# Retention in blocks of 64 tokens on the four quarters of the matrix engine

## Chip, cores, metric

One core of one Trainium2 chip. The metric is the device time of one execution in microseconds (us), the median of several. PE is TensorE, the matrix engine; PEld are its weight loads; VectorE (DVE), ScalarE (ACT) and SP (which issues transfers) are the others.

## The reference, in short

```python
def _attn_ref(q, k, v):                       # (4, 8, 768, 64) each
    for t in range(S):
        state = gamma * state + k[t] (x) v[t] # per batch and head, 64x64
        y[t] = scale * q[t] @ state
# y as (3072 tokens, 512) feeds
h = x @ w_in                                  # 512 -> 2048
g = h * erf(softplus(h))
return g @ w_out                              # 2048 -> 512
```

The retention is the small part. The two large products, done by a scheme with seven products for eight, are the rest. Everything is fp32.

## The kernel before: the parts concerned

The retention is done by chunks of 128 tokens, 24 in all (6 for each of 4 sequences). Keys and queries are scaled so that no decay is left inside a chunk. Each chunk is one visit of PE between two parts of the large products:

```python
# L416, scores of the next chunk: contraction 64, 128 keys x 128 queries
nc.tensor.matmul(pp[s][:, hp, :], KT[j][s*D:(s+1)*D, hp, :], QT[j][s*D:(s+1)*D, hp, :], ...)
# L428, VectorE: causal mask, out of PSUM into SBUF, 2 x (128 x 512)
nc.vector.tensor_tensor(AM[j][:, s], SC[j][s], causal[...].to_broadcast([P, HP, C]), op=ALU.mult)
# L451, state times queries: 64 x 64, 128 columns, on four quarters
nc.tensor.matmul(place(h), state[own, u, :], QT[j][own, u, :], ...)
# L456, values times masked scores: contraction 128, 64 x 128
nc.tensor.matmul(place(h), V[j][:, h, :], AM[j][:, h % 2, h // 2, :], ...)
# L465, state update: contraction 128, 64 x 64
nc.tensor.matmul(new[...], KQ[j][:, 0, h, :], V[j][:, h, :], ...)
... # ScalarE copies the result to XC, VectorE adds `new` to the state
```

The order of one round g in the steady part:

```python
        hidden_part(g, 4)
        hidden_part(g, 3)          # its last read of a PSUM bank is on VectorE (L627)
        if more:
            O_(j)                  # L451, L456, L465
            A(j)                   # VectorE: state
            if j + 1 < NJ:
                S_(j + 1, ps_h)    # L416
                M(j + 1)           # L428
        ...
        for p in (2, 4):
            project_part(g - 1, p) # L674
        gate(g)
```

`ps_h` is a pool of two PSUM banks that the large products and the scores share in turn.

## Time and profile before

| | before |
|---|---|
| median of 3 runs (a fourth makes it 710.75 below) | 710.84 us |
| PE busy | 98% |
| VectorE, ScalarE busy | 53%, 36% |
| one round with a visit / without | 27.97 / 24.60 us |

PE is the bound, so read the chain of waits in order of time: each row is when a piece of PE's program started, how long until the next, which line, how many records (an fp32 matmul leaves two). A round is the distance between two rows of the same line and count.

### The profile page before, as it was taken

To read this page: it belongs to the slowest core of one execution; us is meant where nothing else is said; L and a number is where in the kernel's file an instruction comes from. 1 tells how busy PE (TensorE), PEld (TensorE's weight loads), DVE (VectorE), ACT (ScalarE), POOL (GpSimd) and SP (SyncE) were. 2 spreads that over 40 slices of the span, in tenths; PEclk is the share of its full clock that TensorE was granted. 3 is DMA by queue.
4 is the path that set the end of the run, shared out by engine and by line. 5 is a ranking of instruction groups with operands and counts; after the bars stand their busy time and mean duration, and the time that the engine had idled before them with its cause. 6 is when DMAs were issued, how large, how long until landed. Compare 5 with 4: busy or idle time off the path is not lost.

```text
span 709.3 us, 12055 instructions
## 1 busy us (share of the span) xinstructions
PE 695.8 (98%) x5126; PEld 590.8 (83%) x5126; DVE 379.4 (53%) x532; ACT 256.7 (36%) x289; POOL 6.2 (1%) x19
## 2 busy tenths in 40 slices
PE   8799999999999999999999999999999999999998
PEld 7535444486999998999999999989999999999996
DVE  4599999264854553563554454544553463243234
ACT  3266462325144144243242441441432423414431
POOL 1000000010000000000000000000000000000000
PEclk9999999999999999999999999999999999999999
DMA  9999763102322232211222223230321210000000
GB/s 193 209 255 245 185 193 61 26 1 42 102 38 37 71 60 43 60 32 30 62 42 43 67 37 60 55 59 9 57 57 32 44 48 1 2 30 1 1 30 30
DMA packets 147205, 46.96 MB, mean 66 GB/s; under 512 B 135760, under 2 KB 136016, under 8 KB 147152
## 3 DMA queue, kind: packets, MB, share of 16 engines
q1 hardware_dynamic: 144640, 45.66, 29.5%
q10 hardware_dynamic: 2512, 0.53, 0.5%
q8 instruction: 40, 0.66, 0.4%
q14 instruction: 13, 0.11, 0.1%
HBM read 39.86 MB, written 6.29 MB: 65 GB/s over the span
## 4 chain that ended last, share of the span: by engine, by line
PE 95%; DMA 2%; SPq 1%; DVE 1%; issue 0%; ACT 0%; POOL 0%; DVEq 0%; POOLq 0%
PE hp L602 35%; PE o L674 35%; PE o L545 8%; PE hp L532 7%; PE r L456 3%; PE hp L416 3%; DMA w_in_sb<-in_moe_w_in_dram 2%; PE r L451 1%; PE r L465 1%; PE o L362 1%; PE r L403 1%; SPq L114 1%; PE r L416 1%; SPq L156 0%; DVE am L428 0%
## 5 line engine op out<-in xcount | busy, mean ns | idle before, releaser
L602 PE MATMUL hp<-xs,w_in_sb 128*128 128x128 f32 x1280 | 149.8, 275 | 0.0
L602 PEld LDWEIGHTS hp<-xs,w_in_sb 128*128 128x128 f32 x1280 | 147.8, 192 | 1.6 <-issue 0.5
L674 PE MATMUL o<-w_out_sb,h 128*128 128x256 f32 x640 | 141.7, 379 | 0.0
L674 PEld LDWEIGHTS o<-w_out_sb,h 128*128 128x128 f32 x640 | 121.6, 190 | 16.5
L602 PE MATMUL hp<-xT,w_in_sb 128*128 128x128 f32 x960 | 113.7, 275 | 0.0
L602 PEld LDWEIGHTS hp<-xT,w_in_sb 128*128 128x128 f32 x960 | 111.9, 192 | 1.9 <-issue 1.0
L674 PE MATMUL o<-w_out_sb,e 128*128 128x256 f32 x480 | 112.1, 383 | 0.0
L521 DVE TENSOR_TENSOR e<-h,e 128x1024 f32<-128x1024 f32 x42 | 49.6, 1222 | 101.7 <-ACT e L502 101.7
L674 PEld LDWEIGHTS o<-w_out_sb,e 128*128 128x128 f32 x480 | 88.2, 190 | 12.5 <-PE r L456 0.2
L497 ACT ACT_TABLE_LOAD x24 | 30.8, 1283 | 79.1 <-issue 69.6
L532 PE MATMUL hp<-xT,w_in_sb 128*128 128x512 f32 x128 | 56.7, 596 | 1.8 <-DVE w_in_sb L218 1.4
L627 DVE TENSOR_TENSOR h<-h,hp 128x512 f32<-128x512 f32 x20 | 13.7, 687 | 75.3 <-PE hp L602 75.3
L532 PEld LDWEIGHTS hp<-xT,w_in_sb 128*128 128x128 f32 x128 | 23.8, 190 | 30.9 <-issue 27.7
L502 ACT ACTIVATE e<-e 128x2048 f32<-128x2048 f32 (+1 forms) x23 | 42.1, 1836 | 0.2
L497 ACT ACTIVATE e<-h 128x2048 f32<-128x2048 f32 x22 | 42.0, 1910 | 0.2
L615 DVE TENSOR_TENSOR h<-h,hp 128x512 f32<-128x512 f32 x20 | 13.8, 688 | 51.9 <-PE hp L602 51.9
L470 ACT COPY xT<-r 128x256 f32<-128x256 f32 x44 | 14.4, 375 | 66.7 <-PE r L465 58.9
L625 ACT COPY h<-hp 128x512 f32<-128x512 f32 x20 | 11.7, 585 | 60.3 <-PE hp L602 60.3
L620 ACT COPY h<-hp 128x512 f32<-128x512 f32 x20 | 11.7, 586 | 57.9 <-PE hp L602 57.9
L618 ACT COPY h<-hp 128x512 f32<-128x512 f32 x20 | 11.7, 585 | 55.3 <-PE hp L602 55.3
L502 ACT ACT_TABLE_LOAD x24 | 30.8, 1283 | 0.4
L613 ACT COPY h<-hp 128x512 f32<-128x512 f32 x20 | 11.7, 587 | 48.6 <-PE hp L602 48.6
(102 smaller groups left out, 655.3 us busy)
## 6 DMA issues: line engine op xcount, KB each, us to landing
w_out_sb<-in_moe_w_out_dram SPq DMA_DIRECT2D x14, 512.0 KB, 5.4
kq<-in_k_dram SPq DMA_DIRECT2D x24, 256.0 KB, 3.5
v<-in_v_dram SPq DMA_DIRECT2D x24, 256.0 KB, 3.3
w_in_sb<-in_moe_w_in_dram SPq DMA_DIRECT2D x12, 512.0 KB, 9.4
out_dram<-r SPq DMA_DIRECT2D x23, 256.0 KB, 2.3
kq<-in_q_dram SPq DMA_DIRECT2D x256, 16.0 KB, 1.8
kb<-in_k_dram SPq DMA_DIRECT2D x256, 16.0 KB, 1.7
w_out_sb<-in_moe_w_in_dram SPq DMA_DIRECT2D x4, 512.0 KB, 8.0
```

What stands on the lines that cost most here:

```text
L416: nc.tensor.matmul(pp[s][:, hp, :], KT[j][s * D : (s + 1) * D, hp, :], QT[j][s * D : (s + 1) * D, hp, :], start=True, stop=True,)
L456: nc.tensor.matmul(place(h), V[j][:, h, :], AM[j][:, h % 2, h // 2, :], start=(not c and h % 4 < 2), stop=True, skip_group_check=True,)
L470: nc.scalar.copy(XC[m][:, r::2, i * C : (i + 1) * C], pp[r][:, :2, :])
L497: nc.scalar.activation(E[g], HS[g], AF.Softplus)
L502: nc.scalar.activation(E[g][:, half], E[g][:, half], AF.Erf)
L521: nc.vector.tensor_tensor(E[g][:, half], HS[g][:, half], E[g][:, half], op=ALU.mult)
L532: nc.tensor.matmul(p, w_in_of(ft, kk), XC[0][:, kk, :], start=(kk == 0), stop=(kk == n_k - 1))
L545: nc.tensor.matmul(O[0][tt].rearrange("p (d c) -> p d c", d=2), E[g][:, u * TCH + tt * P : u * TCH + (tt + 1) * P], w_out_of(ft), start=(f ...
L602: nc.tensor.matmul(bank[:, u, :], w_in_sb[:, s, IN[a], kk, u * P : (u + 1) * P], XS[m][b][:, kk, :], start=(p in (1, 2, 5) and u == 0 and ...
L615: nc.vector.tensor_tensor(h["11"], h["11"], flat, op=ALU.add)
L627: nc.vector.tensor_tensor(h["12"], h["12"], flat, op=ALU.add)
L674: nc.tensor.matmul(O[m][i][:, half, :], G[g][a][:, u * P : (u + 1) * P], w_out_sb[:, s, OUT[b], u, :], start=i not in started, stop=(s == ...
```

## The change

The intent: a matmul of 64x64 leaves three quarters of the 128x128 array free, and four of them can run side by side. If every product of a visit is 64x64 with 64 columns, the array changes shape only on the way in and out; and in blocks of 64 tokens the upper-right quarter of the scores, which the mask would zero, is never computed. The price is twice as many matmuls, a state update in the middle of the chunk, and products that cross: where the token half of the keys and the target bank don't match, the values land in other banks ("crossed") and VectorE adds them. From chunk 7 on:

```diff
+    def sub_scores(j):            # 16 matmuls, into columns :D of two banks
+                    SC[j][s][t, hp, :D], KT[j][own, hp, t], QT[j][own, hp, t], start=True, stop=True,
+    def sub_mask(j):              # 2 x (128 x 256)
+                AM[j][:, s, :, :D], SC[j][s][:, :, :D], causal_d[...], op=ALU.mult,
... 
+    def sub_visit(j, g):
+        other = SC[j + 1] = [ret_psum(ps_h) for _ in range(2)]
+        def of_values(crossed):   # 8 matmuls
+                        other[a][own, u % 2, D:] if crossed else pp[a][own, u % 2, t],
+                        V[j][t, 2 * u + r, :], AM[j][t, r, u, :D],
+                        start=crossed or first(r, col), stop=True, skip_group_check=True,
...
+        if c:
+            of_state(0)
+        ...                       # state updates of both blocks, 16 matmuls (8 in a last chunk)
+            nc.vector.tensor_tensor(state, state, new[0], op=ALU.add)
+        of_values(False)
+        if j + 1 < NJ:
+            sub_scores(j + 1)
+            sub_mask(j + 1)
+        of_values(True)
+        of_state(1)
+        ...                       # ScalarE copies, VectorE adds the crossed values and new[1]
-        if more:
+        if more and not first:
+            sub_visit(j, g)
+        elif more:
             O_(j)
             A(j)
-                S_(j + 1, ps_h)
-                M(j + 1)
+            SC[j + 1] = [ret_psum(ps_h) for _ in range(2)]
+            sub_scores(j + 1)
+            sub_mask(j + 1)
```

Line numbers move: L602 becomes L712, L674 becomes L784, L627 becomes L737. New: L485 scores, L492 masks, L520 state times queries, L535 values, L556 state updates, L561 first addition to the state, L576 the addition of the crossed values.

More of the change, by code (lines that the diff above doesn't have):

```diff
@@ L304 @@
     )
+    causal_d = const.tile([P, D], F32, name="causal_d")
+    for r in range(2):
+        own = slice(r * D, (r + 1) * D)
+        nc.gpsimd.tensor_copy(causal_d[own], causal[own, own])
     state = const.tile([P, HP, D], F32, name="state")
@@ L471, in ret_out @@
         pace(2.5)
+    def sub_scores(j):
+        for hp in range(HP):
+            for a, s in itertools.product(range(2), range(2)):
+                t, own = slice(a * D, (a + 1) * D), slice(s * D, (s + 1) * D)
+                nc.tensor.matmul(
+                    SC[j][s][t, hp, :D], KT[j][own, hp, t], QT[j][own, hp, t], start=True, stop=True,
+                )
+    def sub_mask(j):
+        AM[j] = ret.tile([P, 2, HP, C], F32, name="am")
+        for s in range(2):
+            nc.vector.tensor_tensor(
+                AM[j][:, s, :, :D],
+                SC[j][s][:, :, :D],
+                causal_d[:, None, :].to_broadcast([P, HP, D]),
+                op=ALU.mult,
+            )
@@ new lines, in sub_visit, with first, of_state @@
+    def sub_visit(j, g):
+        c = j % NC
+        m, i = divmod(j, JPC)
+        if i == 0:
+            XC[m] = ret.tile([P, HP, TCH], F32, name="xT")
+        pp = [ret_psum() for _ in range(2)]
+        clear = set()
+        def first(*bank):
+            new = bank not in clear
+            clear.add(bank)
+            return new
+        def of_state(a):
+            t = slice(a * D, (a + 1) * D)
+            for u in PAIRS:
+                for r in range(2):
+                    col, own = u // 2, slice(r * D, (r + 1) * D)
+                    nc.tensor.matmul(
+                        pp[r][col * D : (col + 1) * D, u % 2, t], state[own, u, :], QT[j][own, u, t],
+                        start=first(r, col), stop=True, skip_group_check=True,
+                    )
+        other = SC[j + 1] = [ret_psum(ps_h) for _ in range(2)]
+        def of_values(crossed):
+            for u in PAIRS:
+                for a in range(2):
+                    r = 1 - a if crossed else a
+                    col, t = u // 2, slice(a * D, (a + 1) * D)
+                    own = slice(col * D, (col + 1) * D)
+                    nc.tensor.matmul(
+                        other[a][own, u % 2, D:] if crossed else pp[a][own, u % 2, t],
+                        V[j][t, 2 * u + r, :],
+                        AM[j][t, r, u, :D],
+                        start=crossed or first(r, col), stop=True, skip_group_check=True,
+                    )
+        if c:
+            of_state(0)
+        last = chunk_of(g - 1)
+        if (g - G0) % 2 == 1:
+            clear.update((("o", 0), ("o", 1)))
+        new = [
+            O[last][3][:, 1, :].rearrange("p (u d) -> p u d", d=D),
+            pp[1][:, 2:, :].rearrange("p a (b d) -> p (a b) d", d=D),
+        ]
+        adds = range(2) if c < NC - 1 else range(1)
+        for u in range(HP):
+            for r in range(2):
+                for a in adds:
+                    t, h = slice(a * D, (a + 1) * D), 2 * u + r
+                    nc.tensor.matmul(
+                        new[a][r * D : (r + 1) * D, u, :], KQ[j][t, 0, h, :], V[j][t, h, :],
+                        start=first("o" if a == 0 else 1, r), stop=True, skip_group_check=True,
+                    )
+        if c:
+            nc.vector.tensor_tensor(state, state, new[0], op=ALU.add)
+        else:
+            nc.vector.tensor_copy(state, new[0])
+        of_values(False)
[4 more added lines that the diff above has]
+        of_state(1)
+        for r in range(2):
+            a = 1 - r
+            x, y = XC[m][:, r::2, i * C : (i + 1) * C], other[a][:, :2, D:]
+            if c or a:
+                nc.scalar.copy(x, pp[r][:, :2, :])
+                x = x[:, :, a * D : (a + 1) * D]
+                nc.vector.tensor_tensor(x, x, y, op=ALU.add)
+            else:
+                nc.scalar.copy(x[:, :, D:], pp[r][:, :2, D:])
+                nc.scalar.copy(x[:, :, :D], y)
+        if c < NC - 1:
+            nc.vector.tensor_tensor(state, state, new[1], op=ALU.add)
@@ L828 @@
         hidden_part(g, 3)
-        if more:
+        if more and not first:
+            sub_visit(j, g)
+        elif more:
             O_(j)
             A(j)
-            if j + 1 < NJ:
-                S_(j + 1, ps_h)
-                M(j + 1)
+            SC[j + 1] = [ret_psum(ps_h) for _ in range(2)]
+            sub_scores(j + 1)
+            sub_mask(j + 1)
         if g + 1 < NG and (g - G0) % 2:
```

## The prediction

> **What bounds the kernel now.** I read the busy totals first, then the chain of work that ended last, then that chain in order of time around one visit of the retention, then the timeline and the single start times inside one visit.
>
> ```profile
> span 709.3 us, 12055 instructions
> ...
> PE 695.8 (98%) x5126; PEld 590.8 (83%) x5126; DVE 379.4 (53%) x532; ACT 256.7 (36%) x289; POOL 6.2 (1%) x19
> ```
>
> The matrix engine (PE) is busy all the time, VectorE half of it. The chain of waits says the same: 95% of it is PE, in program order. So time is gained only by making the stream of PE shorter, and lost by any hole in it. The retention comes in visits, one per chunk of 128 tokens; the chain in order of time (start us, us, what) shows one whole round with a visit, and a round after the last chunk, without one:
>
> ```profile
> 211.64 3.57 PE hp L602 x32
> 215.21 0.60 PE r L451 x16
> 215.81 1.02 PE r L456 x16
> 216.83 0.46 PE r L465 x16
> 217.30 1.09 PE hp L416 x16
> 218.39 10.56 PE o L674 x48
> ```
> ```profile
> 655.41 3.57 PE hp L602 x32
> 658.98 10.36 PE o L674 x48
> 669.35 8.93 PE hp L602 x80
> 678.28 1.73 PE o L674 x8
> 680.01 3.57 PE hp L602 x32
> ```
>
> L451 is query times state, L456 the masked scores times values, L465 the state update, L416 the next chunk's scores. A visit is 3.18 us, and the L674 block after it takes 10.56 instead of 10.36 us, so a visit costs 3.38 us. The change touches 17 visits (chunks 7 to 23): 57 us, 8% of the span, is all that is at stake.
>
> Each fp32 matmul leaves two records (x16 for 8 matmuls). By records, L465 (two column halves, 64 columns streamed) runs at 0.46/16 = 29 ns, the others at 37 (L451) to 68 ns (L416). The single start times show why. In L451, four quarters of 64x64: starts 243.266, .272, .279, .286, then .375: four within 20 ns, then the next four 109 ns later. In L465: pairs 7 ns apart, every 58.4 ns. At every border between kinds the next group comes some 0.15 us late: L451 is 4 groups x 0.109 = 0.44 us, the other 0.16 us is the change of array shape.
>
> The timeline (start us, us, engine, line) shows what VectorE does meanwhile:
>
> ```profile
> 215.25 0.69 DVE L627 TENSOR_TENSOR h<-h,hp 128x512 f32<-128x512 f32 x1 [3.99 <-PE hp L602]
> ...
> 217.75 0.42 DVE L484 TENSOR_TENSOR state<-state,r 128x256 f32<-128x256 f32 x1 [1.81 <-ACT xT L470]
> ...
> 218.42 1.29 DVE L428 TENSOR_TENSOR am<-hp,causal 128x512 f32<-128x512 f32 x2 [0.25 <-PE hp L416]
> ```
>
> The two masks of the scores (L428) run under the 10.56 us of L674. Nothing waits for them.
>
> **What the Trainium skill says.** "TensorEngine Tiling (Array Packing)", section "Key Properties": a change of tiling mode drains the engine, while tiles of one mode work independently and load weights in parallel. The trace agrees: 0.16 us at a border, four quarters side by side inside L451. "PSUM — Partial Sum Buffer", section "PSUM bank collisions raise a hardware error": guard PSUM by bank and quadrant with semaphores, not by address. This trace has no such wait inside a visit; the changed program has one (below). "TensorE: Matmul & The Clock Gate", section "Wait — 56ns, not 53.3ns?": starts are never closer than about 25 ns, however few columns. The trace differs for starts in different quarters, 7 ns, but in its mean over any eight records it never beats 27 ns, so as a mean rate this is untested. "Runtime: NRT & Kernel Launch", section "Instruction fetch mechanics": a floor of about 20 sequencer cycles per instruction. No stretch of this trace is long and dense enough to show or refute it.
>
> **The change part by part.** Removed per visit: 8 matmuls each of L451, L456, L465 and L416, 64 records in four array shapes. Added: 64 matmuls of 64x64 with 64 columns, 128 records: state times the first 64 queries (16), state updates of both blocks (32), own-block values (16), next scores (32), crossed values (16), state times the last 64 queries (16). Consecutive matmuls go to the four quarters in turn, and the two row halves write different banks. All are of one shape, so only the way in and the way out drain.
>
> PE's own time: 128/4 = 32 groups. A quarter streams 64 columns as in L465, so a group takes 58.4 ns (L465's pitch), if four quarters go side by side as in L451: 32 x 0.0584 = 1.87 us. Way in 0.16, way out 10.56 - 10.36 = 0.20. Sum 2.23 against 3.38 us: 1.15 us gained per visit, about 19 us in all, if nothing waits.
>
> But something waits. The crossed values are written into the unused columns of the very two banks that hold the new scores, directly after these scores. In the built program the first two crossed matmuls each carry a wait for VectorE, and counting VectorE's increments gives which: the first and the second mask of the new scores. Both masks, hidden before, now lie between two matmuls. Cost, from the trace of before:
> - last score matmul's start to the start of the mask: 246.081 to 246.38 = 0.30 us with a 272 ns matmul; with L465's 222 ns form 0.25 us;
> - the masks are 128x256 instead of 128x512: 0.42 us each (L484's form). Two of 0.69 us took 1.29, so the second starts 0.08 before the first ends: 0.34 + 0.42 = 0.76 us;
> - end of a VectorE instruction to PE: 0.055 us (seven starts of PE that a mask released early in the run: 0.053 to 0.057);
> - restart with an empty weight buffer 0.05 us, less the 0.058 us that the next group would have taken anyway.
>
> Sum 1.06 us of hole. The other waits don't bind by these numbers. The scores need L627 to have left their bank: 0.85 us after the visit's start, while PE comes to them after 64 records, 0.16 + 0.93 = 1.09 us. The addition to the state that the last products need is done at about 1.5 us, before the masks. Work moved to VectorE (two additions of 128 elements, one more to the state, smaller masks: +0.4 us a visit) finds it half idle. ScalarE's copies come about 1 us later, and the gate behind them with them; its consumer on PE comes two product blocks later.
>
> So a full visit costs 2.23 + 1.06 = 3.29 us against 3.38. There are 12 of them: -1.1 us. First chunks of a sequence (2) have no state product: 3.29 - 0.47 = 2.82 against 2.58 + 0.20 = 2.78, +0.1 us in all. Last chunks (2) have one update instead of two: 3.06 against 2.91, +0.3. The very last visit has no scores and no mask: 1.8 before, about 1.7 after, -0.1. In the visit ahead of the 17 only the scores change, from 1.09 to 0.16 + 0.47: -0.5. Sum: -1.3 us. The whole gain on the array goes into the wait for the masks; from 710.8 the time comes to 709.5 us.
>
> **The rivals.**
> 1. No wait: had the masks been hidden as before, 16 visits would gain 1.06 us more, 17 us: 692.5, faster by 2.6%. For it: the profile of before, where nothing waits for a mask inside the steady part. Against it: the wait stands in the program. I hold it very unlikely.
> 2. A floor of 25 ns per matmul as a mean, also across quarters. The 96 records ahead of the wait then take 2.40 instead of 1.40 us, the 32 behind it 0.80 instead of 0.47: +1.33 us a visit, +21 us: 731. For it: no stretch of before is denser than 27 ns. Against it: that is just what the array allows there (109/4), and starts are 7 ns apart.
> 3. The sequencer can't feed 256 instructions so fast. The queue holds 64 when the visit starts (the "TensorE" page's opening table); of the 192 ahead of the wait 128 must be fed. At 20 cycles of 1.2 GHz, 16.7 ns: 2.13 us instead of 0.16 + 1.40 = 1.56, and the hole refills the queue for the rest: +0.57 us, +9 us: 718.5. For it: density doubles. Against it: nothing measured here.
> 4. Weights of four quarters load only two at a time: 0.109 us a group, +1.6 us a visit, +26 us: 736. Against it: in L451 the first four loads start at 243.104 to .124 and the next four at 243.159 to .179, 55 ns later in every quarter.
>
> **Range and chances.** I give the sum (709.5) about 60%, rival 3 or a milder feed limit 22%, rivals 2 and 4 together 13%, rival 1 with other gains 5%. The middle of that lies a little above the sum: 711 us, with 704 to 729 to hold it 8 times in 10. Faster by over 2% (below 696.6) 0.05; within 2% 0.75; slower by over 2% (above 725) 0.20.
>
> **What would show each step.** In the chain of the changed kernel: groups of 16 records at 0.23 us (the array step; 0.40 would be rival 2, 0.44 rival 4; groups that start dense and thin out after some 32 pairs, rival 3). A wait of PE for the mask before the crossed values, about 1 us, some 16 times, where before it had none. The L674 block after a visit still 10.56 us. VectorE some 7 us busier, ScalarE the same. I would be wrong if that wait is short or missing, or if the 64x64 matmuls run clearly slower than 14.6 ns a record.

## More of the kernel before

Kernel before, three rounds around the border of a sequence:

```profile
295.54 3.57 PE hp L602 x32
...
323.04 3.57 PE hp L602 x32
...
350.41 3.57 PE hp L602 x32
...
378.37 3.57 PE hp L602 x32
```

The last chunk of a sequence (no state update) makes a round of 27.50 us, the first one (no state product) 27.37, a full one 27.96.

## The result, and the profile after

| | before | after |
|---|---|---|
| median of 4 runs | 710.75 us | 711.91 us |
| range | 710.15 to 711.07 | 711.67 to 712.89 |
| ratio | | 1.002, 95% interval 1.0003 to 1.0037 |

A ratio is the mean time of one kernel's fast runs over that of the other's in the same rounds, so not quite the ratio of the medians quoted. The result is correct and the time the same within 2%.

The busy totals of the page of the changed kernel:

```profile
PE 688.0 (97%) x6214; PEld 583.6 (82%) x6214; DVE 385.3 (54%) x581; ACT 256.9 (36%) x291; POOL 6.6 (1%) x21
```

PE is busy 7.8 us less, but the span of the profiled run is 711.2 instead of 709.3 us: PE now has holes. The chain of waits in order of time, one full round of the changed kernel:

```profile
239.99 3.57 PE hp L712 x32
244.65 0.54 PE hp L485 x32
245.19 0.42 DVE am L492
245.98 0.40 PE hp L535 x11
246.67 10.56 PE o L784 x48
257.23 8.93 PE hp L712 x80
266.16 1.73 PE o L784 x8
267.88 3.57 PE hp L712 x32
```

Two things to see. The round is 267.88 - 239.99 = 27.89 us, against 27.97. And in a chain that held only PE, a mask on VectorE now stands between the scores (L485) and the crossed values (L535). (Only the longest pieces are listed, so short ones leave gaps between rows.) The busy times in the three parts of that visit (us; then for each engine busy us and instructions; the clock) give the sizes:

```profile
243.49:244.92 1.43, 1.43 (x97) 1.43 (x96) 1.11 (x2) 0.00 (x0) 0.00 (x0) 1.00 0.00 0
244.92:245.98 1.06, 0.52 (x18) 0.25 (x8) 0.76 (x2) 0.00 (x0) 0.00 (x0) 1.00 0.21 50
245.98:246.67 0.69, 0.69 (x31) 0.62 (x31) 0.00 (x0) 0.00 (x0) 0.00 (x0) 1.00 1.16 261
```

The columns after the stretch are PE, PEld, DVE, ACT, POOL, then the granted clock, the DMA share and GB/s. First 96 matmul records (and one that was still running) in 1.43 us, dense. Then 1.06 us in which PE starts almost nothing (what it shows as busy is the modelled end of matmuls that had started) and VectorE spends 0.76 us on two instructions, the masks. Then the last 32 records and the way out. The list of waits has it for the whole run (us in total, times, longest):

```profile
PEld hp L535 <- DVE am L492: 10.7, 16, 0.7
PE hp L535 <- DVE am L492: 8.5, 16, 0.5
```

Sixteen times, once in each visit that has scores. The 8.5 us count only time with no matmul in flight; the loss is larger, because a matmul's modelled end covers the first part of each hole and PE restarts with one matmul, then waits again for the second mask.

### The profile page after: what moved, and what is told of

Read it like the earlier page. It is cut to its first block, busy times and chain, and to the rows that moved or that the text cites. A ratio compares the mean times of both kernels' runs of the same rounds, so it can differ in the third digit from the quotient of the medians.

```text
span 711.2 us, 14317 instructions
## 1 busy us (share of the span) xinstructions
PE 688.0 (97%) x6214; PEld 583.6 (82%) x6214; DVE 385.3 (54%) x581; ACT 256.9 (36%) x291; POOL 6.6 (1%) x21
## 4 chain that ended last, share of the span: by engine, by line
PE 90%; DVE 4%; DMA 3%; SPq 1%; issue 1%; ACT 0%; DVEq 0%
PE hp L712 35%; PE o L784 34%; PE o L655 8%; PE hp L642 4%; PE hp L535 2%; DMA w_in_sb<-in_moe_w_in_dram 2%; PE r L520 1%; PE hp L485 1%; DVE am L492 1%; PE o L556 1%; DMA w_out_sb<-in_moe_w_out_dram 1%; SPq L114 1%; DVE w_out_sb L211 1%; DMA kq<-in_q_dram 1%; PE r L535 1%
## 5 line engine op out<-in xcount | busy, mean ns | idle before, releaser
L712 PE MATMUL hp<-xs,w_in_sb 128*128 128x128 f32 x1280 | 149.8, 275 | 0.0
L712 PEld LDWEIGHTS hp<-xs,w_in_sb 128*128 128x128 f32 x1280 | 147.8, 192 | 1.6 <-issue 0.5
L784 PE MATMUL o<-w_out_sb,h 128*128 128x256 f32 x640 | 141.7, 379 | 0.0
L784 PEld LDWEIGHTS o<-w_out_sb,h 128*128 128x128 f32 x640 | 121.6, 190 | 16.5
L712 PE MATMUL hp<-xT,w_in_sb 128*128 128x128 f32 x960 | 113.7, 275 | 0.0
L712 PEld LDWEIGHTS hp<-xT,w_in_sb 128*128 128x128 f32 x960 | 111.9, 192 | 1.9 <-issue 1.0
L784 PE MATMUL o<-w_out_sb,e 128*128 128x256 f32 x480 | 112.1, 383 | 0.0
L784 PEld LDWEIGHTS o<-w_out_sb,e 128*128 128x128 f32 x480 | 88.2, 190 | 11.6
L737 DVE TENSOR_TENSOR h<-h,hp 128x512 f32<-128x512 f32 x20 | 13.7, 686 | 75.3 <-PE hp L712 75.3
L574 ACT COPY xT<-r 128x256 f32<-128x256 f32 x32 | 10.4, 375 | 71.9 <-PE r L520 71.9
```

The costliest lines, as they stand in the source:

```text
L712: nc.tensor.matmul(bank[:, u, :], w_in_sb[:, s, IN[a], kk, u * P : (u + 1) * P], XS[m][b][:, kk, :], start=(p in (1, 2, 5) and u == 0 and ...
L737: nc.vector.tensor_tensor(h["12"], h["12"], flat, op=ALU.add)
L784: nc.tensor.matmul(O[m][i][:, half, :], G[g][a][:, u * P : (u + 1) * P], w_out_sb[:, s, OUT[b], u, :], start=i not in started, stop=(s == ...
```

## The experiments

The theory (W): the array gains 1.15 us a visit as predicted, and the wait of the crossed values for both masks gives 1.06 us of it back. The wait stands in the built program: the crossed values go into the two PSUM banks from which VectorE reads the scores, and the first matmul into each waits for that bank's mask. (No run gives the crossed values banks of their own in the same order, so that the shared bank makes the wait is read from the program, not tested by itself.) Rivals: F, PE's sequencer cannot feed twice as many instructions, and the hole only hides that; N, the wait stands where another one would, for the state. Each is timed beside the kernel before on the same chip: 711.82 us in the first four runs (one chip), 711.46 in the last three (another). Between calls, compare the ratios.

### 1. Crossed values first

```diff
         of_values(False)
+        of_values(True)
         if j + 1 < NJ:
             sub_scores(j + 1)
             sub_mask(j + 1)
-        of_values(True)
         of_state(1)
```

Each crossed matmul is complete by itself, and the scores use other columns, so the order is free. The banks now carry the same data, but the last write of PE to them is the scores, and nobody on PE waits for the masks.

> One edit to the changed kernel: the crossed values are issued before the new scores instead of after them, so nothing on PE has to wait for the masks; the same 64 matmuls, in another order. Theory W (the wait for the masks took the gain): the hole of about 1.08 us goes from 16 visits, 17 us: 694.6 us, 2.3% under the kernel before; a full visit costs 2.23 us instead of 3.30. Rival F (the sequencer cannot feed 256 instructions in 1.9 us, and the hole only hid that, because the queue refilled in it): the visit thins out after some 32 pairs of records and keeps at least half a microsecond of the hole: 703 us or more. Rival N (the wait is only where other waits would show, for VectorE's addition to the state): PE waits for the state ahead of its last 16 records instead, and 708 us or more remain.

Measured: 695.42 us (695.1 to 697.19), ratio 0.9777 (0.9757 to 0.9797), correct. The chain of this kernel, one round:

```profile
264.14 3.57 PE hp L712 x32
267.71 0.39 PE r L520 x16
268.80 0.23 PE hp L535 x16
269.04 0.47 PE hp L485 x32
269.50 0.23 PE r L520 x16
269.74 10.56 PE o L784 x48
280.29 8.93 PE hp L712 x80
289.22 1.73 PE o L784 x8
290.95 3.57 PE hp L712 x32
```

A visit from 267.71 to 269.74 is 2.03 us for 128 records: 0.16 us way in plus 32 groups of 0.0584 us, to the hundredth. The round is 26.81 us, 1.08 less than with the wait. So W holds. F falls: 256 instructions in 2.03 us are fed without a hole. N falls as well: no wait for the state comes in its place. This one edit makes the change worth 2.2% against the kernel before.

### 2. State products between scores and crossed values

```diff
             sub_mask(j + 1)
-        of_values(True)
         of_state(1)
+        of_values(True)
```

> One edit to the changed kernel: the last state products are issued between the new scores and the crossed values, so that PE has 16 records (4 groups of 58 ns) of other work while VectorE masks. Theory W: the hole shrinks by just these 0.23 us in 16 visits, 3.7 us: 708.2 us. Rival F or N: no change beyond 1 us, as the number of instructions and the addition to the state are the same.

Measured: 708.49 us (708.27 to 709.62), ratio 0.9958 (0.9941 to 0.9976). PE's wait for the masks, as the list of waits has it:

```profile
PE hp L535 <- DVE am L492: 4.1, 16, 0.3
```

Still 16 times, half as long. One round:

```profile
238.68 3.57 PE hp L712 x32
...
266.34 3.57 PE hp L712 x32
```

It is 27.66 us against 27.89, 0.23 us shorter: the 16 records of other work moved into the hole shorten it by just their own length, as W says. In 16 rounds that is 3.7 us, as expected. By the ratios of the two kernels 4.4 us were gained (some 1.7 either way), by their medians 3.4.

### 3. Each mask twice

```diff
-        for s in range(2):
+        for s in (0, 0, 1, 1):
```

> The changed kernel with each mask computed twice on VectorE (same values written again). VectorE is 54% busy, so off the path this would cost nothing. Theory W: PE waits for the second of each pair, two more instructions of 0.34 us pitch in 16 visits, 0.68 x 16 = 11 us: 722.8 us, with a hole of about 1.75 us. Rivals F and N: within 2 us of the changed kernel, 712 to 714.

Measured: 738.50 us (735.63 to 741.72), ratio 1.0378 (1.0341 to 1.0415). VectorE, half idle, is on the path, as W says; but the size is more than twice what was expected (+27 us by the medians, +25 by the ratios, instead of +11). Two terms were missing. First, the four masks do not follow each other at the 0.34 us of two masks: in the timeline they take

```profile
246.46 1.67 DVE L492 TENSOR_TENSOR am<-hp,causal_d 128x256 f32<-128x256 f32 x4 [0.28 <-PE hp L485]
```

1.67 us against 0.76 for two, so a round of 28.81 us against 27.90, 0.91 us more: 16 x 0.91 = 14.6 us. Each of the four takes its full 0.42 us, where two overlapped by 0.08; why is not known. Second, some rounds are longer still. In the profiled run (733.8 us, its fastest) five L784 blocks after a visit took 12.24 instead of 10.56 us. The busy times of a normal and of a long block, with the clock in the third column from the right:

```profile
306.51:317.07 10.56, 10.56 (x50) 9.32 (x51) 5.49 (x12) 7.04 (x6) 0.00 (x0) 1.00 0.23 36
335.22:347.46 12.24, 12.24 (x51) 10.50 (x51) 4.00 (x8) 7.10 (x7) 0.00 (x0) 0.86 0.21 34
```

The granted clock is 0.86 in the long one. The trace's clock records show what lies behind it: five stretches of 3.41 us at half clock, each worth 1.7 us. 14.6 + 5 x 1.7 = 23.1 us over the changed kernel's 711.2 makes 734.3, and 733.8 was measured. So in five rounds clock was lost after the hole too. No trace of another kernel here has such a stretch in its visits, and none has so long a hole; that the hole is the cause is argued from this, not tested. It fits the spread of these runs as well (two others have a mean clock of 0.974 and 0.981).

### 4. The same wait in the kernel before

```diff
                 S_(j + 1, ps_h)
                 M(j + 1)
+                for x in SC[j + 1]:
+                    nc.tensor.matmul(x[:, 0, :D], ident, ident[:, :D],
+                                     start=True, stop=True, skip_group_check=True)
```

The dummies overwrite scores that have been read; the result stays correct.

> The kernel before, with two small dummy matmuls (128x128 by 64 columns, 4 records) into the two score banks after the masks have been asked for: the same kind of wait put into the old program. Theory W: the hole there is 0.30 us to the first mask, 1.29 us of masks, 0.05 back to PE, 0.05 restart, and 0.22 us of dummy work, less 0.2 us that the border to the next block costs anyway: about 1.7 us in 17 visits, 29 us: 740 us. If such a wait were mostly hidden by PE's queue: 4 us for the dummy work alone, 715 us.

Measured: 740.28 us (738.32 to 742.43), ratio 1.0412 (1.0387 to 1.0437), the 740 of W. PE's wait appears, twice in each of 17 visits (L838 is the line of the dummies):

```profile
PE hp L838 <- DVE am L428: 16.0, 34, 0.8
```

The wait and the dummies together cost the old kernel 28 us, of which the dummies' own work was expected to be 4; before, the masks were nobody's cost only because nothing of PE's had to follow the masks.

### 5. Without VectorE's additions

```diff
                 nc.scalar.copy(x, pp[r][:, :2, :])
-                x = x[:, :, a * D : (a + 1) * D]
-                nc.vector.tensor_tensor(x, x, y, op=ALU.add)
```

Made from the kernel of run 1. The result is wrong (relative error 0.23).

> The kernel with the crossed values first, without VectorE's additions of the crossed half of the values (the result is wrong on purpose, except in blocks that start a sequence). They take 0.28 us each, two a visit, some 9 us of VectorE's time in all. Theory W says that this moved work lies beside PE: 695.4 us within 1. Rival (VectorE's longer chain after a visit delays the sums that the next product needs): 3 us or more faster, 692 or less.

Measured: 695.24 us (694.26 to 696.21), ratio 0.9773 (0.9759 to 0.9788). Run 1, without the edit, had 0.9777 (on the other chip). So VectorE's additions lie beside PE and cost nothing that these runs can see, about 0.2% (1.5 us).

### 6 and 7. Borders put back, and their control

Both from the kernel of run 1, with one dummy matmul after the first state products, one after the state updates and one after the values:

```diff
+        def border():
+            nc.tensor.matmul(
+                pp[0][:P, 3, :D], ident[:P, :P], ident[:P, :D],   # run 7: D in place of P
+                start=False, stop=True, skip_group_check=True,
+            )
```

> The kernel with the crossed values first, and three small dummy matmuls of 128x128 (64 columns, into an unused part of a bank) put between the kinds of products of a visit, so that the array changes shape again inside the visit: six more borders. By the prediction's numbers each dummy costs 0.20 us out, 0.16 us in and 0.11 us for itself, 0.47 us; 49 of them: 23 us, 718 us. If the borders cost nothing (rival: all the gain comes from the products left out) only the dummies' own time is added: 5 us, 701 us.

> The control of the run with borders: the same three dummy matmuls a visit, but 64x64 on one quarter, the shape of their neighbours. No border, only up to 0.12 us each: 697 to 701 us. If it costs as much as the full-array dummies, these say nothing about borders.

Measured: with full-array dummies 719.55 us (719.5 to 719.65), ratio 1.0115 (1.01 to 1.013); with quarter dummies 699.64 us (699.22 to 701.15), ratio 0.9839 (0.9823 to 0.9856). The chains, first with full-array dummies (one round: 28.39 us), then with quarter dummies (27.15 us); L721 is the line of L712 there:

```profile
239.80 3.57 PE hp L721 x32
...
268.19 3.57 PE hp L721 x32
```
```profile
237.89 3.57 PE hp L721 x32
...
265.04 3.57 PE hp L721 x32
```

Against 26.81 us without dummies, a quarter dummy costs 0.11 us and a full-array one 0.53. The difference, 0.41 us for two changes of shape, is about 0.2 us for each; in the totals, 19.9 us over 49 dummies, also 0.41. So uniform shape is a real part of the gain. Of the 1.15 us that the array gains in a visit, the two inner borders of the kernel before (L451 to L456, L465 to L416) make some 0.35: its four kinds would stream in 4 x 0.109 + 8 x 0.109 + 8 x 0.058 + 8 x 0.112 = 2.67 us (an estimate, with group pitches from its start times), 0.71 less than the 3.38 they cost with four borders, and the changed visit has 0.36 for two. The other 0.8 is shorter streaming, 1.87 instead of 2.67 us.

## Why the prediction was right, and where it was off

It gave 711 us, 704 to 729, "within 2%" at 0.75; 711.9 was measured. Step by step:

- **PE's own time.** Predicted 32 groups of 58.4 ns and 0.16 us way in. Right: run 1 shows 2.03 us. Four quarters load weights and stream side by side at this pitch, for 128 records.
- **The wait for the masks.** Predicted 16 holes of 1.06 us, from reading the waits of the built program and counting which VectorE instruction each stands for. Right: 1.08 us between the rounds with and without it (27.89 and 26.81 us), and runs 1 to 4 show it to be the cause, not a companion.
- **A full visit.** Predicted 3.29 against 3.38 us, 0.09 less; measured 0.07 less by round. Right.
- **VectorE and ScalarE off the path.** Right: run 5 for VectorE's additions; for ScalarE there is no run, but in run 1 PE's steady rounds wait for neither. VectorE is 5.9 us busier (some 7 predicted), ScalarE 0.2.
- **The rivals.** Rival 1 (no wait) did not come: PE waited 16 times. Nor did 2, 3 and 4 (a floor of 25 ns, the feed, weights two at a time): in run 1 the mean is 14.6 ns a record.
- **Two misreadings without effect on the sum.** The four kinds of product of before have three array shapes, not four, and not every border between kinds costs 0.15 us: L456 and L465 have one shape (128x64), and the start at their border comes 0.11 us after the one before, L456's usual pitch.
- **The visits at the borders of a sequence.** Wrong in the working, though small. The rounds of the changed kernel, to be held against the four shown of before:

```profile
295.78 3.57 PE hp L712 x32
...
323.68 3.57 PE hp L712 x32
...
351.47 3.57 PE hp L712 x32
...
379.36 3.57 PE hp L712 x32
```

The last chunk takes 27.90 us, as long as a full one, against 27.50 before: 0.40 us lost, 0.15 predicted. Leaving out one of two updates saves no time, because the other's eight matmuls use only one row half, so two quarters: their records start two every 58 ns, where a full visit starts four. The first chunk takes 27.79 against 27.37: 0.42 us lost, 0.04 predicted. "No state product" was taken as 32 records saved; only the first block lacks it (16 records, 0.23 us), and with less ahead of them the scores come before their bank is free (VectorE's L737 leaves it at 327.97, and the scores start to flow at 328.03): they take

```profile
328.11 0.67 PE hp L485 x32
```

0.67 us there against 0.54 elsewhere. And the very last visit, first before, then after:

```profile
629.00 3.57 PE hp L602 x32
...
655.41 3.57 PE hp L602 x32
```
```profile
630.32 3.57 PE hp L712 x32
634.79 0.43 DVE state L561
...
656.94 3.57 PE hp L712 x32
```

It takes 26.62 against 26.41, since of_state(1) finds no masks to hide VectorE's addition to the state behind: 0.2 us lost, 0.1 gain predicted. The sum over the rounds is then 12 x -0.07 + 2 x 0.42 + 2 x 0.40 + 0.21, and -0.46 for the first visit with new scores only: +0.55 us where -1.3 was predicted. The profile has +0.63 from the round at 156.37 (157.26 after) to that at 680.01 (681.53 after). The sum was thus 1.8 us too low. The mis-sized term is the edge visits: 1.85 us dearer where 0.3 was predicted, so 1.55 of the 1.8; the rest is the full visits, 0.07 us cheaper each instead of 0.09. The profiled run of the changed kernel was also 0.9 us late before all this; in runs 1 to 3 and 5 to 7, whose start is the same program, that row lies anywhere from 156.19 to 157.85, so I take this for the spread from run to run, not for an effect. The "sum" of 709.5 us was a little low, and the 711 lay nearer by luck: it allowed for rivals that did not come, and what made up the difference was the edge visits and the spread.

## What to carry to other kernels

In this program two uses of one PSUM bank tied the engine that reads to the one that writes, though they use disjoint columns: 16 waits of 1.06 us. When a change packs a second use into a bank, put the writes first and the read last, so that nobody needs the bank after the reader. Read the waits of the built program, not only its work: here the whole gain of run 1, 16 us against the kernel before, hung on the order of two calls. And VectorE's work that costs nothing in one kernel cost 4% in run 4 (its dummies included), where the next instruction of the busiest engine came to depend on it.

## What the Trainium skill lacked or had wrong

- "TensorE: Matmul & The Clock Gate", section "Wait — 56ns, not 53.3ns?", has a floor of about 25 ns from start to start. For fp32 records of 64 columns in four quarters the runs show 14.6 ns as a mean over 128 records (run 1), with single starts 7 ns apart. The same page's Part 3, section "The mechanism", does have tiles about 4 ns apart; what is missing is the exception where the floor is told.
- "Runtime: NRT & Kernel Launch", section "Instruction fetch mechanics", has a floor of about 20 sequencer cycles an instruction. Run 1 has 256 matmul and weight-load instructions in 2.03 us, 7.9 ns each; even if 64 of them, the queue's depth by the opening table of "TensorE: Matmul & The Clock Gate", stood ready beforehand, the other 192 came at 10.6 ns. Nothing like the 16.7 ns of the prediction's rival 3 showed on PE. This need not contradict the skill: the section named in the first point says that matmuls and weight loads can be issued without that sequencer's code. The section on fetching should say so beside its floor.
- "TensorEngine Tiling (Array Packing)", section "Key Properties", says that a change of mode drains the engine, without a figure. Runs 6 and 7 show 0.41 us for two changes, about 0.2 us each, for fp32 matmuls.
- "TensorE: Matmul & The Clock Gate", section "🎯 Why this matters for your kernels", warns of PE-idle gaps over about 3 us (its section "A second HAM failure mode: psum-queue depth-cycling" tells of short idles between groups too, without a length). In run 3 a 3.41 us stretch at half clock followed shorter ones: two holes, 0.98 and 0.47 us without a matmul in flight and only one matmul between them, in five of 16 visits. The visits had the same holes; what differed was when they came. The stretches begin on a grid of 3.41 us, and the five are just the visits whose first hole began 0.2 to 0.7 us after a point of it (the others: 0.04, or 0.98 and more). That is one trace, and not a tested rule. The other kernels had no such stretch in the visits; the longest hole of run 4 was 0.78 us and its next 0.16. Where the limit lies between these was not measured.
